# Two token groups side by side in the gate and value products of the last FFN chunks, with a new order

## The chip, the cores and the metric

The kernel runs on one NeuronCore of a Trainium2 chip. The metric is the device time of one execution in microseconds (us); the number that is compared is the median over runs. The engines are TensorE (PE, matrix products; PEld is its weight load), VectorE (DVE), ScalarE (ACT), GpSimd (POOL) and SyncE (SP), whose queue issues the DMAs here. Each runs its own list of instructions in order.

## What is computed

The reference is a linear attention with a complex decay, followed by a gated feed-forward network (FFN), all in fp32:

```python
def _attn_ref(q, k, v, a_re, a_im):          # (4, 8, 768, 48) each
    mag = np.sqrt(a_re * a_re + a_im * a_im)
    scale = np.minimum(mag, 0.999) / (mag + 1e-06)
    ...
    for t in range(S):
        new_re = ar * S_re - ai * S_im
        new_im = ar * S_im + ai * S_re
        kv = np.einsum('bhd,bhe->bhde', k[:, :, t], v[:, :, t])
        S_re, S_im = (new_re + kv, new_im)
        y[:, :, t] = np.einsum('bhd,bhde->bhe', q[:, :, t], S_re)

def _moe_ref(x, w_gate, w_val, w_out):       # x (3072, 384), d_ff 1536
    g = x @ w_gate
    silu = g * (1.0 / (1.0 + np.exp(-g)))
    val = x @ w_val
    return (silu * val @ w_out).astype(np.float32)
```

## The kernel before

**Tiling.** The 3072 tokens are 24 slabs of 128 (four batches, six pieces of the sequence). Two slabs make a group, so there are 12 groups of 256 tokens. `stage_ops(g)` prepares a group's decays, keys and queries, mostly on DVE and ACT. `slab_ops(n)` does the attention of slab n. From slab 6 on, DVE transposes its keys and queries (L650) into a spare weight tile, twelve DMAs carry that into a T tile (L659, steps sh0 to sh3; the T tag has two buffers), and PE makes the scores (`sc`, L692 into p_ps), the product with the state (`st`) and the product with the values (`V`, L692 into p_py). Between scores and values DVE multiplies with the mask (`mk`, L720). ACT copies the result, rounded, to xh (`evh`, L781); DVE makes the rest, xl (`evl`, L788). Two groups' xh and xl fit at a time.

**FFN.** `ffn_ops(g)` runs the FFN of a group in 12 chunks f of 128 hidden units. f1 (L943) makes gate and value of 256 tokens in one PSUM bank, p_gv (two of these): 18 products of 256 columns. Each fp32 operand stands as a high and a low part of the type fp32r, so a product is three: high x high, high x low, low x high, over three k-tiles. Group 0 uses plain fp32 and has 6 products instead of 18. Then follow silu on ACT (`th`, L949), the product with the value on DVE (`h2`, L954), the split of the result into `hh` (DVE or ACT) and `hl` (DVE), and f2 (L977), six products of 384 columns that add to the group's two PSUM banks p_po. After chunk 11 the two halves are copied to ost (two buffers) and stored (L991). A chunk or slab is named by group and number: f1_10.1 is chunk 1 of group 10, sc0_23 the first half of slab 23's scores.

**Weights.** At the start the weight words are converted on DVE and split into high and low parts (casts `c4` on DVE or ACT, rests `c5` on DVE). In the rest of the program the weights are read again and their range is looked at (`kl`, `k1`, `k2`, L891 to L900).

**What sets the order.** All steps are added to a `Planner`. It gives each engine, step by step, the ready step with the earliest due time (`key`, plus an entry in the table `NUDGE`), with its own prices for the steps, and then the program is written out in that order. Where a step may run on more than one engine, the planner also picks that. So constants at the head of the file move instructions anywhere in the program.

```python
pl.add("f1_" + I, {"PE": 2.16 if g else 2.6}, f1, ...)
pl.add("f2_" + I, {"PE": 1.06 if g else 1.31}, f2, ...)
slots = dict(qs=1, ks=1, T=2, dec=3, sc=2, sg=2, hh=2, hl=2, ost=2, xh=2, xl=2, vt=2, vr=2,
             gv=2, po=1, ps=2, py=1, pm=1)
```

Of the kernel before, what the change touches and what calls it, by code (L numbers as in the profile page):

```python
# [33 lines left out]
SWITCH_KEY = 6.4577  # L34
RUSH, WARY = 100.0, 8.0
CALM_S, CALM_C, CALM_T, CALM_A, CALM_D = 3.5883, 1.0641, 0.128, 0.29, 0.2775
LATE, WARY2, WARY3, WARY4 = 2.1401, 2.0386, 1.7902, 0.0841
STRETCH = 1.757
AHEAD, YIELD, QUEUED = -15.9216, 13.0268, 5.6794
T0, PER, FT, FT0 = 49.2709, 22.663, 4.032, 4.936  # L40
LEAD0, LEAD2 = 8.1674, 2.0456
CONV0, CONVP = 32.3335, 40.5772
T1 = T0 + 12 * FT0
CK0, CKP = 169.077, 13.465
RCP, SQR = 1, 2
NUDGE = {
# [13 lines left out]
SHY = -5.6765  # L60
POOL_FROM = 9.8274
# [169 lines left out]
def quick(ctx, tc, q, k, v, a_re, a_im, w_gate, w_val, w_out, out, count):  # L231
# [89 lines left out]
    def new(tag, inst):  # L321
# [6 lines left out]
        else:  # L328
# [7 lines left out]
            if tag in ("xh", "xl", "hh", "hl"):  # L336
# [591 lines left out]
    def ffn_ops(g):  # L928
        t0, step = (T1 + (g - 1) * NF * FT, FT) if g else (T0, FT0)
        for f in range(NF):  # L930
            I = f"{g}.{f}"
            key = t0 + f * step

            def f1(e, f=f, I=I):
                xh, xl = at_["xh", g], at_.get(("xl", g))
                gv = new("gv", I).rearrange("p (i t) -> p i t", i=2)
                for i, nm in enumerate(("g", "v")):
                    wh, wl = (weight(nm, f, x) for x in ((HIGH, LOW) if g else (WHOLE, WHOLE)))
                    mm = []
                    for kt in range(KT):  # L940
                        mm += [(wh[:, kt, :], xh[:, kt, :])] if g == 0 else [(wh[:, kt, :], xh[:, kt, :]), (wh[:, kt, :], xl[:, kt, :]), (wl[:, kt, :], xh[:, kt, :])]
                    for m, (l, r) in enumerate(mm):
                        nc.tensor.matmul(out=gv[:, i, :], lhsT=l, rhs=r, start=(m == 0), stop=(m == len(mm) - 1))  # L943
            pl.add("f1_" + I, {"PE": 2.16 if g else 2.6}, f1,
                   deps=[f"ev{'l' if g else 'h'}{2 * g + i}" for i in range(2)] + [f"c{5 if g else 3}{f}w", f"f1_{g}.{f - 1}", f"f1_{g - 1}.{NF - 1}"],
                   alloc=[("gv", I)], use=[("xh", g), ("xl", g)] if g else [("xh", g)], key=key)

            def silu(e, I=I):
                nc.scalar.activation(out=new("sg", I), in_=at_["gv", I][:, 0:2 * P], func=AF.Silu)  # L949
            pl.add("th_" + I, {"ACT": 0.28}, silu, deps=["f1_" + I], alloc=[("sg", I)], use=[("gv", I)], table="silu")  # L950

            def h2(e, I=I):
                sg = at_["sg", I]
                nc.vector.tensor_tensor(out=sg, in0=sg, in1=at_["gv", I][:, 2 * P:4 * P], op=ALU.mult)  # L954
            pl.add("h2_" + I, {"DVE": 0.34}, h2, deps=["th_" + I], use=[("sg", I), ("gv", I)])

            def hh(e, I=I):
                cast(e, new("hh", I), at_["sg", I])
            if g > 0:
                pl.add("hh_" + I, {"DVE": 0.2, "ACT": 0.28}, hh, deps=["h2_" + I], alloc=[("hh", I)], use=[("sg", I)], port=True)  # L960

            def hl(e, I=I):
                tt(e, new("hl", I), at_["sg", I], at_["hh", I].bitcast(F32), ALU.subtract)
            if g > 0:
                pl.add("hl_" + I, cost(("DVE", "POOL"), 2 * P), hl, deps=["hh_" + I], alloc=[("hl", I)], use=[("sg", I), ("hh", I)])

            def f2(e, f=f, I=I):
                hh, hl, h = (at_.get((x, I)) for x in ("hh", "hl", "sg"))
                products = ((hh, HIGH), (hh, LOW), (hl, HIGH)) if g else ((h, WHOLE),)
                if f == 0:  # L970
                    new("po", f"{g}.0")
                    new("po", f"{g}.1")
                for i in range(2):
                    cs = slice(i * P, (i + 1) * P)
                    po = at_["po", f"{g}.{i}"][:, :DM]
                    for j, (l, part) in enumerate(products):
                        nc.tensor.matmul(out=po, lhsT=l[:, cs], rhs=weight("o", f, part),  # L977
                                         start=f == 0 and j == 0, stop=f == NF - 1 and j == len(products) - 1)
# [259 lines left out]
```

## Time and profile before

| | |
|---|---|
| median of 3 runs | 627.1 us (626.94 to 627.57) |
| span of the profiled execution | 625.2 us |
| PE busy | 599.1 us, 96% |
| PE weight loads busy | 565.9 us, 91% |
| DVE busy | 501.6 us, 80% |
| ACT busy | 405.2 us, 65% |

The profile shows one execution. The weight load overlaps the products, so the two rows of PE are not added. Matmul records follow each other pipelined: a record of 280 ns may start 114 ns after the one ahead of it, so what a product costs is read from the distance of starts, or from a block's time in the chain of waits divided by its products. The median stands 1.9 us above the profiled span.

### The profile page before, as it was taken

Reading aid. Unit: us, or ns where it says so; the run is one execution under the profiler, and the core shown is the slowest. Engines: PE = TensorE matmul, PEld = TensorE weight load, DVE = VectorE, ACT = ScalarE, POOL = GpSimd, SP = SyncE. Lnnn points to the kernel's source line nnn. Section 1 sums busy time; section 2 is a strip of 40 time slices with the busy share of each in tenths; the row PEclk is TensorE's granted clock in tenths of the full one; section 3 lists DMA queues with packets and bytes.
Section 4 is the critical chain, followed back from the end, with each engine's and each line's share of the span. In section 5 each row is a group of like instructions: output and inputs, shape, how many; then the busy total and the mean of one; then the engine's idle time right before and its main releaser. Section 6 shows DMA issues by size and latency. Waiting matters only on the chain.

```text
span 625.2 us, 16113 instructions
## 1 busy us (share of the span) xinstructions
PE 599.1 (96%) x6562; PEld 565.9 (91%) x6562; DVE 501.6 (80%) x931; ACT 405.2 (65%) x653; POOL 4.2 (1%) x15
## 2 busy tenths in 40 slices
PE   2699999999999999999999999999999999999996
PEld 1488788989999999999999999999999999999995
DVE  8999999999978788977979869769869768544432
ACT  7953548887895885957876966966966874212210
POOL 2000000000000000000000000000000000000000
PEclk9899999999999999999999999999999999999998
DMA  7899701334544564455356354554463542331100
GB/s 257 230 280 296 246 27 33 65 123 123 142 118 124 141 153 119 129 141 127 101 144 161 114 140 108 143 142 107 132 170 103 155 109 70 102 104 51 52 1 30
DMA packets 155574, 79.89 MB, mean 128 GB/s; under 512 B 116187, under 2 KB 151261, under 8 KB 155494
## 3 DMA queue, kind: packets, MB, share of 16 engines
q1 hardware_dynamic: 155494, 78.80, 46.0%
q8 instruction: 53, 0.87, 0.6%
q14 instruction: 27, 0.22, 0.1%
HBM read 59.83 MB, written 4.78 MB: 103 GB/s over the span
## 4 chain that ended last, share of the span: by engine, by line
PE 79%; DVE 12%; DMA 3%; SPq 3%; issue 1%; ACT 1%; DVEq 0%
PE p_gv L943 41%; PE p_po L977 21%; PE p_py L692 6%; PE p_ps L692 5%; DVE ww L350 2%; PE p_pm L503 2%; PE p_pm L761 2%; DVE sg L954 1%; PE p_pm L758 1%; DMA wo<-in_q_dram 1%; SPq L681 1%; DVE s L350 1%; DVE ks L350 1%; DVE wo L350 1%; PE p_gv L630 1%
## 5 line engine op out<-in xcount | busy, mean ns | idle before, releaser
L943 PE MATMUL p_gv<-xh,ww 128*128 128x256 f32 x1596 | 303.3, 288 | 2.0 <-DVE sg L954 1.4
L943 PEld LDWEIGHTS p_gv<-xh,ww 128*128 128x128 f32 x1596 | 256.0, 189 | 9.2 <-DVE sg L954 2.9
L943 PE MATMUL p_gv<-xl,ww 128*128 128x256 f32 x726 | 201.3, 277 | 0.0
L1069 ACT ACT_TABLE_LOAD x118 | 151.4, 1283 | 2.1
L943 PEld LDWEIGHTS p_gv<-xl,ww 128*128 128x128 f32 x726 | 136.3, 188 | 0.2 <-issue 0.2
L949 ACT ACTIVATE sg<-p_gv 128x256 f32<-128x256 f32 x144 | 55.1, 385 | 122.1 <-PE p_gv L943 120.8
L977 PE MATMUL p_po<-wo,hh 128*128 128x384 f32 x484 | 125.1, 339 | 0.0
L954 DVE TENSOR_TENSOR sg<-sg,p_gv 128x256 f32<-128x256 f32 x144 | 59.0, 412 | 56.0 <-ACT sg L949 55.7
L977 PEld LDWEIGHTS p_po<-wo,hh 128*128 128x128 f32 x484 | 81.2, 188 | 1.6 <-issue 1.6
L977 PE MATMUL p_po<-wo,hl 128*128 128x384 f32 x242 | 80.8, 334 | 0.6 <-DVE hl L350 0.6
L350 DVE TENSOR_TENSOR hl<-sg,hh 128x256 fp32r<-128x256 f32 x132 | 54.8, 416 | 7.0 <-ACT hh L354 1.8
L977 PEld LDWEIGHTS p_po<-wo,hl 128*128 128x128 f32 x242 | 45.4, 188 | 0.9 <-DVE hl L350 0.9
L407 ACT ACTIVATE s<-s 128x768 f32<-128x768 f32 x44 | 36.7, 843 | 9.7 <-DVE s L350 6.7
L692 PEld LDWEIGHTS p_ps<-T 96*64 96x64 f32 x768 | 35.9, 138 | 5.0 <-issue 2.2
L692 PE MATMUL p_ps<-T 96*64 96x128 f32 (+1 forms) x768 | 39.4, 254 | 0.0
L720 DVE TENSOR_TENSOR sc<-p_ps,turn 128x512 f32<-128x512 f32 x48 | 31.8, 684 | 3.7 <-PE p_ps L692 3.5
L781 ACT CAST xh<-p_py 128x384 fp32r<-128x384 f32 x22 | 10.6, 480 | 33.9 <-PE p_py L692 33.8
L354 ACT CAST hh<-sg 128x256 fp32r<-128x256 f32 x45 | 18.1, 405 | 18.5 <-DVE sg L954 14.7
L356 DVE CAST hh<-sg 128x256 fp32r<-128x256 f32 x87 | 25.1, 290 | 6.1 <-PE p_po L977 2.5
L692 PE MATMUL p_py<-sc,vr 128*32 128x128 f32 x384 | 26.1, 273 | 0.0
L692 PE MATMUL p_py<-sc,vt 128*32 128x128 f32 x384 | 25.0, 273 | 0.0
L943 PE MATMUL p_gv<-xh,ww-1_292 128*128 128x256 f32 x132 | 24.9, 280 | 0.0
(146 smaller groups left out, 852.3 us busy)
## 6 DMA issues: line engine op xcount, KB each, us to landing
T<-ww SPq DMA_DIRECT2D x216, 64.0 KB, 2.1
wo<-in_moe_w_out_dram SPq DMA_DIRECT2D x24, 384.0 KB, 4.7
ww<-in_moe_w_gate_dram SPq DMA_DIRECT2D x12, 384.0 KB, 5.9
ww<-in_moe_w_val_dram SPq DMA_DIRECT2D x12, 384.0 KB, 6.9
vt<-in_v_dram SPq DMA_DIRECT2D x24, 192.0 KB, 4.0
out_dram<-ost SPq DMA_DIRECT2D x24, 192.0 KB, 2.2
wo<-in_moe_w_gate_dram SPq DMA_DIRECT2D x12, 384.0 KB, 5.4
wo<-in_moe_w_val_dram SPq DMA_DIRECT2D x12, 384.0 KB, 3.5
```

Of the source, the lines that this page charges most:

```text
L350: V[e].tensor_tensor(out=out, in0=a, in1=b, op=op)
L354: nc.scalar.copy(out=out, in_=in_)
L356: nc.vector.tensor_copy(out=out, in_=in_)
L407: nc.scalar.activation(out=of(to or dst), in_=of(source), func=func, scale=scale, **kw)
L503: nc.tensor.matmul(out=ps, lhsT=tri, rhs=flat(half(x, i)), start=j == 0, stop=j == 1)
L692: nc.tensor.matmul(out=o, lhsT=l, rhs=r, start=opens, stop=closes, tile_position=(0, width * slot), skip_group_check=True)
L720: nc.vector.tensor_tensor(out=s.rearrange("p (r m) t -> p r m t", m=2), in0=scores[qd].rearrange("p (r m) t -> p r m t", m=2), in1=m, op=A ...
L943: nc.tensor.matmul(out=gv[:, i, :], lhsT=l, rhs=r, start=(m == 0), stop=(m == len(mm) - 1))
L949: nc.scalar.activation(out=new("sg", I), in_=at_["gv", I][:, 0:2 * P], func=AF.Silu)
L954: nc.vector.tensor_tensor(out=sg, in0=sg, in1=at_["gv", I][:, 2 * P:4 * P], op=ALU.mult)
L977: nc.tensor.matmul(out=po, lhsT=l[:, cs], rhs=weight("o", f, part), start=f == 0 and j == 0, stop=f == NF - 1 and j == len(products) - 1)
L1069: nc.scalar.preload_act_table_set(op.load)
```

## The change

Chunks 0, 1 and 11 of groups 10 and 11 stay as they are. For chunks 2 to 10 (`PAIRED`) both groups are taken together. The xh of both groups are copied side by side into a T tile that attention no longer needs, and the same for xl (`both`, two copies each). The gate of a chunk (f1g) is nine products of 512 columns into one p_gv bank, the value (f1v) nine into the other. silu, h2, hh and hl then work on 512 columns and use the tiles of the staged attention (re, im, s1, s2, s3, qt) in place of sg, hh and hl. f2 stays at 384 columns, one step for each group. Group 10 adds up in p_po, group 11 in the two banks that held the scores. The table of due times and nudges is another one throughout.

```diff
+PAIRED = (2, 11)
...
 NUDGE = {
-    "sadd0.1": -5.6, "cumF1.1": 3.8, "mk1_3": 15.5, "c32w": 4.0, "c110w": 3.4, "f1_0.2": -12.1, "h2_0.5": 9.1,
...
+    "cumF1.1": 6.6, "c32w": 4.9, "r05": 61.6, "qs1_5": -10.4, "ld_im6": -43.0, "kz1s0": -46.3, "f2_9.0": 28.7,
...
+            if tag == "T" and isinstance(inst, str):
+                t = work.tile([P, math.prod(shape[1:])], F32R, name=inst, tag=tag, bufs=slots[tag])
+                t = t[:, INPUT:INPUT + KT * 4 * P].rearrange("p (k n) -> p k n", k=KT)
...
+    last = NGRP - 2, NGRP - 1
+    tail = [((g,), f) for g in last for f in range(PAIRED[0])] + [(last, f) for f in range(*PAIRED)]
+    tail += [((g,), f) for g in last for f in range(PAIRED[1], NF)]
...
+    def sums(g, i):
+        return scores[i].rearrange("p h t -> p (h t)")[:, :DM] if g == last[1] else at_["po", f"{g}.{i}"][:, :DM]
...
+        def gated(x, parity):
+            if many == 1:
+                return new(x, I)
+            tag, inst = {"sg": (("re", "im"), "sg"), "hh": (("s1", "s2"), "him"), "hl": (("s3", "qt"), "lim")}[x]
+            t = new(tag[parity], (inst, I))
+            at_[x, I] = flat(t)[:, GATED:GATED + wide]
+            return at_[x, I]
...
+        def product(nm, o):
+            xh, xl = (at_["xh", g], at_.get(("xl", g))) if many == 1 else (at_["T", x] for x in ("both xh", "both xl"))
+            wh, wl = (weight(nm, f, x) for x in ((HIGH, LOW) if g else (WHOLE, WHOLE)))
+            mm = []
+            for kt in range(KT):
+                mm += [(wh[:, kt], xh[:, kt])] if g == 0 else [(wh[:, kt], xh[:, kt]), (wh[:, kt], xl[:, kt]), (wl[:, kt], xh[:, kt])]
+            for m, (l, r) in enumerate(mm):
+                nc.tensor.matmul(out=o, lhsT=l, rhs=r, start=(m == 0), stop=(m == len(mm) - 1))
...
+            gate, value = ("gv", I + "gate"), ("gv", I + "value")
+            made = []
+            for i, x in enumerate(("gate", "value")):
+                made.append(pl.add(f"f1{x[0]}_" + I, {"PE": 2.05}, lambda e, i=i, x=x: f1_wide(e, i, x), deps=ready + made,
+                                   alloc=[(gate, value)[i]], use=inputs_, key=key + 2 * i))
...
+    def both(x):
+        for n, g in enumerate(last):
+            def copy(e, n=n, g=g):
+                if n == 0:
+                    new("T", "both " + x)
+                cast(e, at_["T", "both " + x][:, :, 2 * P * n:2 * P * (n + 1)], at_[x, g])
...
+    def ffn_tail(before):
+        for x in ("xh", "xl"):
+            both(x)
+        t = T1 + (NGRP - 3) * NF * FT
+        for gs, f in tail:
+            ffn_ops(gs, f, t, before)
+            t += FT * len(gs)
+            if f == NF - 1:
+                rows_out(gs[0], t + 4, before)
```

**PE, the chunks of the last groups.** Before, one chunk (f1, then f2 of the chunk ahead; L943 is f1, L977 f2):

```order
L943 MATMUL p_gv<-xh,ww_1140 128x256
L943 MATMUL p_gv<-xl,ww_1140 128x256
L943 MATMUL p_gv<-xh,ww_1140 128x256 x2
...
L977 MATMUL p_po<-wo_1127,hh 128x384 x2
L977 MATMUL p_po<-wo_1127,hl 128x384
```

Now, chunk 3's gate (L977 is f1 here, L1037 f2; p_ps are the score banks, in which group 11 adds up), behind group 11's f2 of chunk 1 and chunk 2's value:

```order
L1037 MATMUL p_ps_98<-wo_900,hh 128x384 x2
L1037 MATMUL p_ps_98<-wo_900,hl 128x384
...
L977 MATMUL p_gv<-both xh,ww_855 128x512
...
L977 MATMUL p_gv<-both xh,ww_879 128x512
L977 MATMUL p_gv<-both xl,ww_879 128x512
L977 MATMUL p_gv<-both xh,ww_879 128x512 x2
```

A gate or a value is nine instructions of 512 columns, 162 in all, where 324 of 256 stood; behind f1g of a chunk comes f2 of the chunk ahead for group 10, behind f1v the same for group 11. The whole tail of PE now reads, by the steps' names: sc and V of slab 22, f2_10.0, f1_10.1, sc and V of slab 23, f2_10.1, f1_11.0, f1_11.1, f2_11.0, f1g of chunk 2, f2_11.1, f1v, f1g of chunk 3, f2 of chunk 2 for group 10, f1v, and so on to f1v of chunk 10; then f1_10.11, f1_11.11 and the f2 that are left. Before, slab 22 stood behind f1_10.3 and slab 23 behind f1_10.7. The transposes of slab 22 stood behind f1_9.9 on DVE's side of the plan, now they stand ahead of f1_9.7.

**DVE, around slab 23's masks** (L720, now L726, into sc). Before:

```order
L954 TENSOR_TENSOR sg<-sg,p_gv 128x256
L720 TENSOR_TENSOR sc<-p_ps_98,turn 128x512
L720 TENSOR_TENSOR sc<-p_ps_99,turn 128x512
L895 TENSOR_REDUCE flags<-wo_1384 128x1
L788 TENSOR_TENSOR xl<-p_py,xh 128x3x128
```

Now:

```order
L1011 TENSOR_TENSOR sg<-sg,p_gv 128x256
L362 CAST hh<-sg 128x256
L356 TENSOR_TENSOR hl<-sg,hh 128x256
L726 TENSOR_TENSOR sc<-p_ps_98,turn 128x512
L726 TENSOR_TENSOR sc<-p_ps_99,turn 128x512
L901 TENSOR_REDUCE flags<-wo_1384 128x1
L794 TENSOR_TENSOR xl<-p_py,xh 128x3x128
L362 COPY both xl<-xl 128x3x256
```

The chunk whose f1 stands ahead of the scores has its hh and hl ahead of the masks now, and behind them before.

**DVE, the end.** Before (p_po_7857 is the second half of group 11's sums):

```order
L954 TENSOR_TENSOR sg_8160<-sg_8160,p_gv_8131 128x256
L356 CAST hh_8171<-sg_8160 128x256
L1014 CAST count_58<-p_pm_8163 1x1
L350 TENSOR_TENSOR hl_8174<-sg_8160,hh_8171 128x256
L356 COPY ost_8184<-p_po_7857 128x384
```

Now (p_po_7338 is the second half of group 10's sums, p_ps1 of group 11's):

```order
L1011 TENSOR_TENSOR sg_7924<-sg_7924,p_gv_7895 128x256
L362 CAST hh_7933<-sg_7924 128x256
L362 COPY ost_7937<-p_po_7338 128x384
L356 TENSOR_TENSOR hl_7940<-sg_7924,hh_7933 128x256
L1102 CAST count_58<-p_pm_7942 1x1
L362 COPY ost_7952<-p_ps1_99 128x384
```

Group 10's last copy came into the last chunk's steps; before, group 10 was stored nine chunks earlier. On SP the last two stores are that of ost_7952 (second half, copied by DVE) and then that of ost_7954 (first half, copied by ACT); before, the first half's went first. The two ost buffers are taken in turn: ost_7952 follows group 10's first half, ost_7954 its second.

**The start.** Up to the FFN of group 2 the order of PE is nearly the same. In what the planner gave to DVE or ACT, the casts of five 384-column and two 768-column weights, three hh and one T copy went from DVE to ACT, and two, three, one and one went from ACT to DVE.

## Rows read from the trace of the kernel before

**Rows 1.** The page's first section: busy us (share of the span) xinstructions.

```profile
PE 599.1 (96%) x6562; PEld 565.9 (91%) x6562; DVE 501.6 (80%) x931; ACT 405.2 (65%) x653; POOL 4.2 (1%) x15
```

**Rows 2.** Busy time by stretch: length, each engine's (instructions), granted clock, DMA share, GB/s.

```profile
30.00:170.00 140.00, 137.40 (x1278) 120.51 (x1274) 138.16 (x241) 94.81 (x147) 0.00 (x0) 1.00 0.52 150
225.00:450.00 225.00, 225.00 (x2828) 220.26 (x2828) 187.45 (x350) 168.76 (x256) 0.00 (x0) 1.00 0.50 130
450.00:550.00 100.00, 99.94 (x1190) 97.52 (x1189) 74.03 (x135) 59.96 (x109) 0.00 (x0) 1.00 0.44 118
550.00:600.00 50.00, 50.00 (x457) 49.60 (x456) 22.00 (x58) 10.07 (x29) 0.00 (x0) 1.00 0.19 59
```

**Rows 3.** PE's waits from 150 to 620 us: total us, times, longest.

```profile
PE p_gv L943 <- DVE sg L954: 1.4, 2, 0.9
```

**Rows 4.** Chain that ended last: start us, us, what (group 0's f1; slab 23; a chunk).

```profile
65.67 2.59 PE p_gv L943 x12
...
562.31 1.55 PE p_ps L692 x24
563.86 1.93 PE p_py L692 x64
...
567.04 2.06 PE p_gv L943 x18
569.10 1.04 PE p_po L977 x6
```

**Rows 5.** DVE by form, 30 to 170 us: xcount | busy us, mean ns | idle before.

```profile
L356 DVE CAST wo<-wo 128x384 fp32r<-128x384 f32 x7 | 2.4, 350 | 0.0
L356 DVE CAST ww<-ww 128x768 fp32r<-128x768 f32 x4 | 2.2, 544 | 0.0
L356 DVE CAST hh<-sg 128x256 fp32r<-128x256 f32 x7 | 2.0, 280 | 0.0
L650 DVE STREAM_TRANSPOSE ww<-ks 128x768 f32<-128x768 f32 x1 | 1.0, 965 | 0.0
```

**Rows 6.** Timeline around slab 23: start us, us, engine, line, what [idle before, releaser].

```profile
562.77 0.42 DVE L954 TENSOR_TENSOR sg<-sg,p_gv 128x256 f32<-128x256 f32 x1 [1.40 <-ACT sg L949]
563.22 1.39 DVE L720 TENSOR_TENSOR sc<-p_ps,turn 128x512 f32<-128x512 f32 x2
...
565.73 0.61 PE L977 MATMUL p_po<-wo,hh 128*128 128x384 f32 x2
565.86 0.48 ACT L781 CAST xh<-p_py 128x384 fp32r<-128x384 f32 x1 [2.59 <-PE p_py L692]
...
566.37 0.56 DVE L788 TENSOR_TENSOR xl<-p_py,xh 128x384 fp32r<-128x384 f32 x1 [1.30 <-ACT xh L781]
...
566.90 0.29 DVE L356 CAST hh<-sg 128x256 fp32r<-128x256 f32 x1
...
567.29 0.43 DVE L350 TENSOR_TENSOR hl<-sg,hh 128x256 fp32r<-128x256 f32 x1
```

**Rows 7.** Timeline of SP's queue: slab 22's twelve copies, the last nine of slab 23's.

```profile
530.92 8.63 SPq L659 DMA_DIRECT2D T<-ww  x12
...
549.04 6.45 SPq L659 DMA_DIRECT2D T<-ww  x9
```

**Rows 8.** The page's DMA issues: KB each, median us from issue to landing.

```profile
T<-ww SPq DMA_DIRECT2D x216, 64.0 KB, 2.1
```

**Rows 9.** Timeline of the end (columns as in rows 6).

```profile
615.32 0.28 PE L943 MATMUL p_gv<-xh,ww 128*128 128x256 f32 x1
...
616.58 0.29 DVE L356 CAST hh<-sg 128x256 fp32r<-128x256 f32 x1
...
619.06 1.34 SPq L991 DMA_DIRECT2D out_dram<-ost  x2
619.07 0.56 DVE L356 COPY ost<-p_po 128x384 f32<-128x384 f32 x1 [1.75 <-PE p_po L977]
```

**Rows 10.** The 24 stores of L991, from issue to landing.

```profile
DMA to landing us min/median/max: 1.9/2.2/6.5
```

More of the change, by code (lines that the diff above doesn't have):

```diff
@@ L59 @@
 HIGH, LOW, WHOLE = 0, 1, 2
-SHY = -5.6765
-POOL_FROM = 9.8274
+SHY = -83.4065
+POOL_FROM = -45.6425
 TABLES = {"exp": ("exp_and_others", "natural_log_exp_and_others"), "ln": ("natural_log_exp_and_others",),
@@ L925, in sector_ops @@
             pl.add(f"km{i}{N}", STT2, least, deps=[f"kz{i}{N}"], use=parts, key=key)
[L928 to L967, printed above, removed]
@@ new lines, in banks, with ffn_ops, home, f1 @@
+    def banks(g):
+        return [("ps", f"sums{i}") for i in range(2)] if g == last[1] else [("po", g)]
+    def ffn_ops(gs, f, key, before):
+        g, many = gs[0], len(gs)
+        I = name(gs, f)
+        wide = 2 * P * many
+        def gated(x, parity):
[5 more added lines that the diff above has]
+            return at_[x, I]
+        def home(x):
+            if many == 1:
+                return x, I
+            tag, inst = {"sg": (("re", "im"), "sg"), "hh": (("s1", "s2"), "him"), "hl": (("s3", "qt"), "lim")}[x]
+            return tag[f % 2], (inst, I)
+        def product(nm, o):
[6 more added lines that the diff above has]
+                nc.tensor.matmul(out=o, lhsT=l, rhs=r, start=(m == 0), stop=(m == len(mm) - 1))
+        def f1(e):
+            gv = new("gv", I).rearrange("p (i t) -> p i t", i=2)
+            for i, nm in enumerate("gv"):
+                product(nm, gv[:, i, :])
+            at_["gate", I], at_["value", I] = gv[:, 0], gv[:, 1]
+        def f1_wide(e, i, x):
+            at_[x, I] = new("gv", I + x)
+            product("gv"[i], at_[x, I])
+        ready = [f"ev{'l' if g else 'h'}{2 * g_ + i}" for g_ in gs for i in range(2)] + [f"c{5 if g else 3}{f}w"] + before["f1"]
+        inputs_ = [(x, g) for x in ("xh", "xl")[:2 if g else 1]]
+        if many > 1:
+            inputs_ = [("T", "both " + x) for x in ("xh", "xl")]
+            ready += [f"both {x}{g_}" for x in ("xh", "xl") for g_ in gs]
+        if many == 1:
+            gate = value = ("gv", I)
+            product_ = pl.add("f1_" + I, {"PE": 2.16 if g else 2.6}, f1, deps=ready, alloc=[gate], use=inputs_, key=key)
+            made = [product_] * 2
+        else:
+            gate, value = ("gv", I + "gate"), ("gv", I + "value")
[3 more added lines that the diff above has]
+                                   alloc=[(gate, value)[i]], use=inputs_, key=key + 2 * i))
+        def silu(e):
+            nc.scalar.activation(out=gated("sg", f % 2), in_=at_["gate", I], func=AF.Silu)
+        pl.add("th_" + I, {"ACT": 0.28 if many == 1 else 0.5}, silu, deps=[made[0]], alloc=[home("sg")], use=[gate], table="silu")
+        def h2(e):
+            sg = at_["sg", I]
+            nc.vector.tensor_tensor(out=sg, in0=sg, in1=at_["value", I], op=ALU.mult)
+        pl.add("h2_" + I, {"DVE": 0.34 if many == 1 else 0.61}, h2, deps=["th_" + I, made[1]], use=[home("sg"), value])
+        def hh(e):
+            cast(e, gated("hh", f % 2), at_["sg", I])
+        def hl(e):
+            tt(e, gated("hl", f % 2), at_["sg", I], at_["hh", I].bitcast(F32), ALU.subtract)
+        if g > 0:
+            pl.add("hh_" + I, {"DVE": 0.2, "ACT": 0.28} if many == 1 else {"DVE": 0.34, "ACT": 0.51}, hh,
+                   deps=["h2_" + I], alloc=[home("hh")], use=[home("sg")], port=True)
+            pl.add("hl_" + I, cost(("DVE", "POOL"), wide), hl, deps=["hh_" + I], alloc=[home("hl")], use=[home("sg"), home("hh")])
+        made_ = []
+        for n, g_ in enumerate(gs):
+            opens, closes = (steps(g_)[x] == (gs, f) for x in (0, -1))
+            def f2(e, n=n, g_=g_, opens=opens, closes=closes):
@@ L976, in f2 @@
                     for j, (l, part) in enumerate(products):
-                        nc.tensor.matmul(out=po, lhsT=l[:, cs], rhs=weight("o", f, part),
-                                         start=f == 0 and j == 0, stop=f == NF - 1 and j == len(products) - 1)
-            PO = [("po", g)]
-            pl.add("f2_" + I, {"PE": 1.06 if g else 1.31}, f2,
-                   deps=([f"hl_{I}", f"c5{f}o"] if g else [f"h2_{I}", f"c3{f}o"]) + ([f"f2_{g}.{f - 1}"] if f else []),
-                   alloc=PO if f == 0 else [], use=([("hh", I), ("hl", I)] if g else [("sg", I)]) + (PO if f else []), key=key + 3)
+                        nc.tensor.matmul(out=sums(g_, i), lhsT=l[:, cs], rhs=weight("o", f, part),
+                                         start=opens and j == 0, stop=closes and j == len(products) - 1)
@@ L1049, in quick @@
         weight_ops(f)
-    ffn_ops(0)
+    before = {"f1": []}
+    ffn_group(0, before)
     for f in range(NF):
@@ L1060, in quick @@
         range_ops(f)
-    for g in range(1, NGRP):
-        ffn_ops(g)
+    for g in range(1, last[0]):
+        ffn_group(g, before)
+    ffn_tail(before)
     verdict_ops()
```

56 lines of the change are left out of this document (36 added, 20 removed), and 12 rows, old and new, of the table NUDGE.

## The prediction

> **What bounds the kernel now.** I read the page's busy shares first: TensorE (PE) is busy 96% of the span, VectorE (DVE) 80% [rows 1]. A share is a mean over stages, so the next view is the busy time by stretch [rows 2]. It shows two regimes. From 30 to 170 us DVE is busy 138.16 of 140 us: that stretch lasts as long as DVE's list of work. From 225 us on PE is busy all the time (225.00 of 225, and 50.00 of 50 near the end), the granted clock is 1.00 there (the 2.4 GHz level), and DVE has 17 to 56% to spare. The view of waits agrees: after 150 us PE waits 1.4 us in all, twice [rows 3]. So after 170 us time changes by what PE has to execute and by new waits of PE. The chain of waits gives PE's prices [rows 4]: a chunk's 18 gate and value products of 256 columns (f1) take 2.06 us, its 6 output products of 384 columns (f2) 1.04, a slab's scores 1.55 and its states and values 1.93. The profiled execution spans 625.2 us; the median of the three timed runs is 627.1, 1.9 above it. I add each change to 627.1.
>
> **The 512 columns.** Chunks 2 to 10 of groups 10 and 11 were 18 f1 blocks of 18 products, 324 products of 256 columns in 18 x 2.06 = 37.1 us, or 114 ns each. They become 162 products of 512. No 512-column product is in the trace. Lower bound: in group 0 the operands are plain fp32, and each f1 product leaves two records (12 records for 6 instructions). They follow each other in 2.59 / 12 = 216 ns [rows 4], which is about what 512 columns take at one column a cycle of 2.4 GHz (213 ns). Upper bound: the 384-column products take 1.04 / 6 = 174 ns, in proportion 232 ns for 512. I take 217, the fp32 row's price, for this reason: where PE never waits, its weight loads are busy 49.60 of 50 us [rows 2], so a product of 256 columns seems to wait for its weights, and a longer one would not. Gain: 37.1 - 162 x 0.217 = 1.9 us. At 216 it is 2.1, at 232 it is a loss of 0.5.
>
> The rows give 114 ns for 256 columns, 228 for two of them. The Trainium skill (TensorE: Matmul & The Clock Gate, Back-to-back issue gap) gives an isolated product N / 2.4 + 2.5 ns: 109 for 256 and 216 for 512. By that rule alone two short products cost 218 and the gain would be 162 x 2.7 ns = 0.4 us, an estimate from that page. The trace's 114 contradicts its first half; whether the second holds for these operands no run here shows yet.
>
> **What comes with them.** The silu, product and splits of a wide chunk work on 512 columns. Their lengths can at most double: on DVE h2 0.42, hh 0.29, hl 0.43 [rows 6], so 2.3 us, 2.7 with the gaps between. The order puts one f2 and the next chunk's gate product (1.04 + 1.95) between a value product and the f2 that needs its hl, so this is hidden. Only for chunk 2 there is the gate product alone, 1.95 us, and of its f2 the first two products need hh only: 0 to 0.4, taken as 0.1. The four copies that lay both groups' xh and xl side by side ("both") are ACT and DVE work of under 1 us each (a cast of 768 columns is 0.54 on DVE [rows 5]). Two f1 and one f2 of group 11 (5.2 us) stand between them and the first wide product. If that cover were gone, they would cost some 2 us.
>
> **What moves: slabs 22 and 23.** The wide chunks need both groups' tokens, so 22 f1 and 23 f2 now follow slab 23's value product, where 16 and 19 did: 6 x 2.06 + 4 x 1.04 = 16.5 us of PE work. Slab 23's scores come that much earlier. Before, its twelve copies into T were issued by 555.5 and landed 2.1 us later, at 557.6 [rows 7, 8], 4.6 us before its scores at 562.2 [rows 4]. In the new order slab 22's transposes stand at f1 of chunk 9.7, and 7 f1, 8 f2 and two slabs (29.7 us) separate that from slab 23's scores. In these must go, by my placing from the rows: transposes done at 1.5, twelve copies 8.6, landing 2.1; slab 23's transposes behind hl of chunk 9.9, at 14.8 to 16.8 (0.97 each [rows 5]); copies and landing until 27.5. Some 2 us remain. On DVE about 9 us of group 11's stage moves ahead of slab 21. Between 450 and 550 DVE idles 26 us of 100 [rows 2], so there is room, but its load before slab 21 rises from 83% to some 95%. I add 0.2 us for short waits, with 0 to 2.5 as bounds.
>
> **Slab 23's mask.** DVE's order now has hh and hl of chunk 10.1 ahead of the masks; before, only h2 stood there. Before, h2 ended at 563.19 and the masks 563.22 to 564.61, and the values ran to 565.73 [rows 6]. With 0.29 + 0.43 and their gaps of 0.1 the masks end 0.7 to 0.95 later, and the second half of the values (from about 565.25) waits 0.1 to 0.35. Taken: 0.3. Then group 11's f1 wants xh and xl: they were ready at 566.93, 1.2 us after the values [rows 6], and f2 of chunk 10.1 covers 1.04 of that and f1's first product the rest: 0.
>
> **The last stores.** Group 10's outputs now close two f2 before group 11's. There are two ost buffers, so each last copy waits until a store of group 10 has landed, and the order of the last two stores is turned round. Count from the start of the last f1 product (615.32 before [rows 9]). DVE's hh ended at 1.55; the copy of group 10's second half now stands behind it (0.56), so its store goes out at 2.14 and lands after 2.2 (least 1.9 [rows 10]), at 4.34. Then ACT's last copy, 0.48 as the 384-column cast [rows 6], and the last store is issued at 4.85. Before, it was issued when DVE's copy was done, 619.63, at 4.31. Cost 0.5 us; 0.2 with the shortest landing, 1.2 if the two stores delay each other by 0.6.
>
> **The ramp.** Between 30 and 170 us, where DVE sets the time, the new plan gives five 384-column and two 768-column weight casts, three hh and one T copy to ACT, and takes two, three, one and one back: net 3 x 0.35 + 2 x 0.28 - 0.54 = 1.1 us less on DVE [rows 5]. PE's order up to there is nearly the same. The recorded lengths overlap a little, so I take 0.8 us. Bounds: 1.7 gained, 0.5 lost, since the places of many steps shift too.
>
> **Sum.** -1.9 + 0.1 + 0.2 + 0.3 + 0.5 - 0.8 = -1.6 us, so 627.1 becomes 625.5.
>
> **Rivals.** (1) *Eaten up.* The 1.9 us are there, but the ramp gives nothing and the new waits come at their upper bounds: -1.9 + 0.4 + 0.35 + 1.2 + 0.2 = +0.2, so 627.3. For it: three of the waits are new in the order and need no bad luck. Against it: all at once. (2) *A 512-column product costs as the 384-column one does*, 232 ns: +0.5 in place of -1.9, so 628.0. For it: all 384-column products here, whatever they read, take 174 ns and not 163. Against it: the fp32 row. (3) *Slower: slab 23 comes late.* Its scores wait for T, because DVE's transposes for slabs 22 and 23 slip. My account leaves 2 us, so each microsecond of slip beyond 2 is one lost; with the other terms at -1.6, a slip of 5 us gives 628.5 and of 6 us 629.5. For it: 83% to 95% load on DVE and one queue (SP) for the 24 copies, the check loads and the stores. Against it: from 225 to 450 us DVE ran at 83% with PE never idle. (4) That the products stay 256 wide is out: the built order shows 162 of 512.
>
> **How the numbers follow.** A measurement here can tell about 0.2%, 1.25 us, from no change: 625.85 and 628.35. The forecast (624 to 626.5) has 0.50; it straddles the lower mark, and I put 0.43 below it. Rival 1 has 0.26, rival 2 0.08, both within the marks; rival 3 has 0.16, of which 0.13 beyond the upper one. So faster has 0.43, same 0.07 + 0.26 + 0.08 + 0.03 = 0.44, slower 0.13; the forecast itself is the likeliest case. Range: from 623.8 (512 columns at 216 ns, ramp 1.7, the waits 0.5 together) to 628.4, which takes in rivals 1 and 2 and part of 3.
>
> **What would show it.** In the new profile: wide f1 products 215 to 220 ns apart and 1.95 us a block (232 ns would be rival 2). PE idle at slab 23's scores with T or the transposes as the releaser (rival 3), or only at its values, for 0.3 us, with the mask as the releaser (forecast). The last store issued 4.5 to 5.5 us after the last f1 product. The chain leaving DVE near 169 us in place of 170. I am wrong if PE is idle more than 2 us in all after 230 us, or if the stretch up to 170 us got longer.

## The result and the profile after

The changed kernel takes 630.6 us (630.45 to 631.2, four runs) against 627.2 for the kernel before on the same chip: a ratio of 1.0059, 95% interval 1.0047 to 1.0072, so 3.5 us slower by the medians where 1.6 us faster was forecast, and above the upper end of the stated range, 628.4. The profiled execution spans 628.8 us, 3.6 more than before. The page's first section and the busy time by stretch, in the columns of [rows 1, 2]:

```profile
PE 600.3 (95%) x6400; PEld 560.4 (89%) x6400; DVE 499.6 (79%) x909; ACT 391.8 (62%) x634; POOL 4.2 (1%) x15
```

```profile
30.00:170.00 140.00, 137.17 (x1277) 121.03 (x1274) 137.63 (x238) 91.92 (x147) 0.00 (x0) 1.00 0.53 151
225.00:450.00 225.00, 224.71 (x2818) 219.54 (x2817) 188.18 (x350) 162.62 (x252) 0.00 (x0) 1.00 0.50 127
...
550.00:600.00 50.00, 50.00 (x278) 43.89 (x272) 18.05 (x39) 10.20 (x23) 0.00 (x0) 1.00 0.13 40
```

The picture of the two regimes is the same. The last row holds the first surprise: between 550 and 600 us the weight loads (PEld) fell from 49.60 busy microseconds to 43.89, as was meant, and PE is as busy as ever. The chain of waits around slab 23 and the first wide blocks says what that bought (to be read beside [rows 4]):

```profile
547.19 1.55 PE p_ps L698 x24
548.74 2.21 PE p_py L698 x64
550.96 1.24 PE p_po L1037 x6
552.20 4.19 PE p_gv L977 x36
556.39 1.04 PE p_ps L1037 x6
557.43 2.10 PE p_gv L977 x9
559.53 1.05 PE p_ps L1037 x6
560.58 4.20 PE p_gv L977 x18
```

Nine products of 512 columns take 2.10 us, 233 ns each, and not 1.95. A gate and a value block, 18 products, take 4.20 us. 36 products of 256 columns, as many as such a pair replaces, take 2 x 2.06 = 4.12 by [rows 4]; the fourth line, 4.19, is group 11's f1 of chunks 0 and 1, still 256 columns wide, which lose 0.08 us at the first product with xl (xl was just ready then).

To place the rest I compare ends of steps before which TensorE has the same work in both kernels, or correct for f1 and f2 that have changed sides at 2.06 and 1.04 us. Up to slab 6's values the changed kernel is 0.2 us ahead (191.9 against 192.1). The 1532nd step of both plans is f1 of chunk 7.5, and the 1532 steps up to there are the same set; it starts at 414.92 us in the changed kernel and 413.48 in the one before: 1.4 behind. At slab 22's values it is still 1.4, at slab 23's 1.7. From there to the last product of the output the changed kernel loses 0.9 more (2.6), and from that product to the end of the span 1.1 (7.5 against 6.5 us). So: **order 1.4, slab 23 0.3, wide chunks 0.9, end 1.1**, 3.6 in all.

### The profile page after: what moved, and what is told of

Same layout as the page of the kernel before. It is cut to its first block, busy times and chain, and to the rows that moved or that the text cites. A ratio compares the mean times of both kernels' runs of the same rounds, so it can differ in the third digit from the quotient of the medians.

```text
span 628.8 us, 15712 instructions
## 1 busy us (share of the span) xinstructions
PE 600.3 (95%) x6400; PEld 560.4 (89%) x6400; DVE 499.6 (79%) x909; ACT 391.8 (62%) x634; POOL 4.2 (1%) x15
## 4 chain that ended last, share of the span: by engine, by line
PE 83%; DVE 9%; ACT 3%; DMA 2%; issue 2%; SPq 1%; DVEq 0%; ACTq 0%
PE p_gv L977 43%; PE p_po L1037 20%; PE p_py L698 6%; PE p_ps L698 6%; PE p_pm L767 2%; PE p_pm L509 2%; PE p_ps L1037 2%; PE p_gv L636 2%; DVE ww L356 1%; DVE sg L1011 1%; ACT L1159 1%; PE p_pm L764 1%; DVE s L356 1%; DMA dr<-qs 1%; DVE ks L356 1%
## 5 line engine op out<-in xcount | busy, mean ns | idle before, releaser
L977 PE MATMUL p_gv<-xh,ww 128*128 128x256 f32 x1380 | 263.8, 289 | 3.1 <-DVE sg L1011 2.5
L977 PEld LDWEIGHTS p_gv<-xh,ww 128*128 128x128 f32 x1380 | 222.5, 189 | 10.4 <-DVE sg L1011 4.0
L977 PE MATMUL p_gv<-xl,ww 128*128 128x256 f32 x618 | 171.6, 278 | 0.0
L977 PEld LDWEIGHTS p_gv<-xl,ww 128*128 128x128 f32 x618 | 116.1, 188 | 0.0
L1037 PE MATMUL p_po<-wo,hh 128*128 128x384 f32 x404 | 104.6, 340 | 0.0
L1011 DVE TENSOR_TENSOR sg<-sg,p_gv 128x256 f32<-128x256 f32 x126 | 51.3, 411 | 30.8 <-ACT sg L1006 30.0
L1037 PEld LDWEIGHTS p_po<-wo,hh 128*128 128x128 f32 x404 | 68.3, 188 | 1.4 <-issue 1.2
L1037 PE MATMUL p_po<-wo,hl 128*128 128x384 f32 x202 | 67.6, 335 | 0.0
L1037 PEld LDWEIGHTS p_po<-wo,hl 128*128 128x128 f32 x202 | 37.9, 188 | 0.1
L977 PE MATMUL p_gv<-both xh,ww 128*128 128x512 f32 x108 | 36.7, 395 | 0.0
L726 DVE TENSOR_TENSOR sc<-p_ps,turn 128x512 f32<-128x512 f32 x48 | 31.8, 686 | 3.5 <-PE p_ps L698 3.3
L906 ACT ACTIVATE wo<-wo 128x384 f32<-128x384 f32 x36 | 20.0, 556 | 9.2 <-DMA wo<-in_moe_w_gate_dram 5.7
```

Of the source, the lines that this page charges most:

```text
L726: nc.vector.tensor_tensor(out=s.rearrange("p (r m) t -> p r m t", m=2), in0=scores[qd].rearrange("p (r m) t -> p r m t", m=2), in1=m, op=A ...
L906: nc.scalar.activation(out=high(0), in_=high(1), func=AF.Square, accum_out=flags[:, fl_hi + j:fl_hi + j + 1])
L977: nc.tensor.matmul(out=o, lhsT=l, rhs=r, start=(m == 0), stop=(m == len(mm) - 1))
L1011: nc.vector.tensor_tensor(out=sg, in0=sg, in1=at_["value", I], op=ALU.mult)
L1037: nc.tensor.matmul(out=sums(g_, i), lhsT=l[:, cs], rhs=weight("o", f, part), start=opens and j == 0, stop=closes and j == len(products) - 1)
```

## Experiments

All times are against the kernel before, run on the same chip between the runs of the experiment. Differences in us are the ratio's distance from 1 times 627; where the medians say something else, both stand. Offsets in a single trace are good to about half a microsecond at best: of kernels with the same order some are 0.9 us later than others already when slab 0 ends (34 us), before any step of the change. That end goes with TensorE's granted clock, which rises while the first groups' products run: it stays at 1.00 (the 2.4 GHz level) from 26.8 to 28.4 us on in the traces whose slab 0 ends at 33.8 to 34.2 us, and from 28.5 to 29.3 us on in those where it ends at 34.4 to 34.9.

### The same weights, two halves

```diff
-                nc.tensor.matmul(out=o, lhsT=l, rhs=r, start=(m == 0), stop=(m == len(mm) - 1))
+                for c in range(0, wide, 2 * P):
+                    nc.tensor.matmul(out=o[:, c:c + 2 * P], lhsT=l, rhs=r[:, c:c + 2 * P],
+                                     start=(m == 0 and c == 0), stop=(m == len(mm) - 1 and c + 2 * P >= wide))
```

> The changed kernel, but each product of 512 columns is issued as two of 256 with the same weights, one behind the other; order, tiles and all other work as in the changed kernel. Theory C (a product of this type costs by its columns, 0.46 ns each, whatever its weights do): the halves follow each other in 114 ns, a pair of blocks takes 4.10 us in place of 4.20, 162 x 5 ns = 0.8 us come back, 629.8 us. Rival W (the 233 ns are the wide operand's own price: it lies in a longer tile and is written by other casts): the halves read the same tile and take 116 to 117 ns each, 630.6 us. Rival L (a short product waits for its weight load, as the prediction took it): the halves take 114 ns, but a second half whose weights are there already is shorter, and the time falls by more than 0.8 us.

Ratio 1.0035 (1.0022 to 1.0047), 2.2 us above before, where the changed kernel was 3.7 above by its ratio; by the medians it is 2.7 and 3.5. So 0.8 to 1.5 us came back, and the time alone does not tell theory C from rival L. The chain of this run, and two rows of its timeline inside a block:

```profile
558.24 2.06 PE p_gv L978 x18
560.30 1.04 PE p_ps L1038 x6
561.34 4.10 PE p_gv L978 x36
```

```profile
561.01 0.36 PEld L978 LDWEIGHTS p_gv<-both xh,ww 128*128 128x128 f32 x2
561.18 0.40 PE L978 MATMUL p_gv<-both xh,ww 128*128 128x256 f32 x2
```

36 short products take 4.10 us where 18 long ones took 4.20, and from slab 23's values to the last product the trace is 0.8 us shorter. That is theory C's price: one wide product costs 5 ns more than two narrow ones. The second pair of rows shows what the edit does not do: each half loads its weights again (324 loads for 324 products here, 162 for 162 in the changed kernel). So half as many loads save nothing, which is shown; what two products would gain from one load that they share is not tested by this run or by any later one.

### What a product costs

> The changed kernel, with the gate and value products of chunks 3 to 8 of the last two groups issued in other cuts, all with the same order of work: chunk 3 as 2 x 256 columns, 4 as 384 + 128, 5 as 4 x 128; chunks 6, 7 and 8 on bf16 views of the same data (the upper halves of the words, so these three chunks' gates and values are computed from coarser numbers) as 512, 2 x 256 and 4 x 128. It is a measure of prices, its time is no result. Theory C (a fp32r product costs 0.455 to 0.467 ns a column at any width): 512 columns 233 ns, 256 114, 384 + 128 174 + 58, 128 columns 58. Rival L (a product takes at least the 110 ns that a weight load takes): 128 columns about 110 ns each. On bf16: if the price belongs to the type, 512 columns take 213 to 216 ns, 256 107 to 109; if it belongs to the place or to the weight loads, 233 and 114 as before.

The chain again; the blocks are chunk 2's gate (nine of 512), chunk 3's value (2 x 256), chunk 4's gate (384 + 128), chunk 5's gate (4 x 128), and the bf16 blocks of chunks 6, 7 and 8 (512, 2 x 256, 4 x 128):

```profile
558.20 2.11 PE p_gv L982 x9
...
566.65 2.05 PE p_gv L982 x18
...
569.75 2.54 PE p_gv L982 x18
...
577.00 3.97 PE p_gv L982 x36
...
590.24 2.06 PE p_gv L982 x9
...
593.34 2.06 PE p_gv L982 x18
...
599.55 2.12 PE p_gv L982 x36
```

Two things are seen. In bf16 the weight loads of 128 x 128 follow each other every 59 ns (2.12 / 36), and yet a bf16 product of 256 columns takes 114 ns, as the fp32r product does. So in bf16 it is not the weights that set 114, and the same price in fp32r speaks against them there too. And the fp32r product of 128 columns takes 110 ns and not 58: below 256 columns something else sets it, and theory C alone is too simple. The next run tells what.

> The changed kernel with nine products more ahead of each wide gate and value block of chunks 3 to 9, whose sums are overwritten by the block. They tell width of the weights from width of the columns (weights x columns): chunk 3 128 x 128, chunk 4 64 x 128, chunk 5 32 x 128, chunk 6 32 x 256, chunk 7 128 x 192, chunk 8 32 x 512, chunk 9 128 x 320. Its time is no result. Theory L' (a fp32r product takes the longer of its columns, 0.45 ns each, and its weight load, 110 ns for 128 weight columns): 128 x 128 110 ns, 64 x 128 and 32 x 128 58 ns, 32 x 256 114, 128 x 192 110, 32 x 512 233, 128 x 320 146. Theory N (fp32r products under 256 columns run at a lower rate whatever the weights): 128 columns 110 ns with 32 weight columns too, 192 columns 165 or 110.

The added products have a line of their own, L980, nine to a block; in order 128 x 128, 64 x 128, 32 x 128, 32 x 256, 128 x 192, 32 x 512, 128 x 320:

```profile
563.40 0.95 PE p_gv L980 x9
...
571.70 0.54 PE p_gv L980 x9
...
579.16 0.53 PE p_gv L980 x9
...
586.63 1.05 PE p_gv L980 x9
...
595.00 0.98 PE p_gv L980 x9
...
603.27 2.08 PE p_gv L980 x9
...
613.74 1.32 PE p_gv L980 x9
```

That is 106, 60, 59, 117, 109, 231 and 147 ns. With 64 or 32 weight columns, 128 columns cost 60; with 128 weight columns, 128 and 192 columns both cost 106 to 109; at 256 and 512 columns 32 weight columns are no cheaper (117 and 231) than 128 (114 and 233). Theory L' holds in all seven: **a fp32r product takes the longer of its columns at about 0.455 ns and its weight load of about 108 ns**. The two meet at some 240 columns (an estimate, 108 / 0.455), so the 256 columns of the kernel before were already past the point from which a weight load is hidden.

The Trainium skill has this number (TensorE: Matmul & The Clock Gate, LDWEIGHTS): a load takes its weight columns divided by 1.2 ns, 107 for 128. The 106 measured here agrees. Set beside the 114 of [rows 4], it would have taken away my reason to expect a gain.

### The order and the pairing, one at a time

The constants and the table of nudges are exchanged between the two kernels, nothing else.

> The kernel before with the constants and the table of nudges of the changed kernel, and no wide products. Its planned order is that of the changed kernel on TensorE up to f1 of chunk 7.5 (about 390 us), and the end has before's form. Theory O (the order that came with the change loses 1.2 to 1.5 us before 390 us by itself, and the wide products and the end the rest): 628.3 to 628.8 us. Rival (the order costs nothing, the whole loss is made where the wide products are): 627.2 us. What the prediction took: the ramp gains 0.8, 626.4 us.

> The changed kernel with the constants and the table of nudges of the kernel before. Its planned order is that of the kernel before on TensorE up to f2 of chunk 8.2 (about 430 us); the pairing stands behind it. Theory C and O: the stretch up to 430 us is as before, the wide products cost 0.75 us, the stores at the end 0.5 to 1.1, slab 23's masks 0 to 0.3: 628.4 to 629.4 us. Rival (the wide products gain 1.9 and only the order lost): 625.5 to 626.5 us. If the order of the changed kernel was needed for the pairing, slab 23 comes late and the time is over 630.

The new table alone: 1.0076 (1.0059 to 1.0094), 4.8 us lost, more than any theory had. Up to f1 of chunk 7.5 it is as expected (414.79 us without the sum that stands ahead of it here, 1.3 behind). Then comes a wait of 2.8 us for a h2 up to 502 us, in a stretch where this kernel's order is that of neither kernel, and it costs more than its length. During the wait TensorE's granted clock falls from 1.00 to 0.50 (the 1.2 GHz level), and the f1 behind it takes 4.21 us in place of 2.06; with the scores (2.40 for 1.55) that is 3.0 us more. The clock is the last number but two of the first row:

```profile
501.30:508.10 6.80, 6.03 (x42) 5.81 (x44) 4.62 (x10) 1.84 (x5) 0.00 (x0) 0.50 0.86 194
```

```profile
502.07 4.21 PE p_gv L945 x18
```

So the total says nothing of the changed kernel. The pairing alone: 1.025 (1.023 to 1.027), 16 us. Its longest wait of TensorE from 530 to 600 us, SP's queue before it, and the chain behind it (slab 23):

```profile
PE p_ps L696 <- DMA T<-ww: 5.7, 1, 5.7
```

```profile
547.45 6.67 SPq L663 DMA_DIRECT2D T<-ww  x9
```

```profile
555.91 2.79 PE p_ps L696 x24
558.70 3.29 PE p_py L696 x64
```

The last nine copies of slab 23's T are issued until 554.1 and slab 23's scores wait 5.7 us for them. Here too the granted clock falls during the wait (0.50 from 554.6 to 561.4 us, the 1.2 GHz level), and slab 23 takes 6.1 us in place of 3.5. Four waits for h2 after 150 us make 3.8 us, where the kernel before has 1.4 in two. Together that is 10.7 us of the 16 lost; the wide products and a later end bring some 3 more, and the rest is not placed. The wait for T is rival 3 of the prediction, in this order and not in that of the changed kernel: the pairing needs slab 23 some 15 us earlier, and of the orders tried here only the new table's gets it there in time. What that costs elsewhere is the next question.

### The end and the masks

```diff
+    for what, ahead_of in (("hh_10.1", "V23"), ("hl_10.1", "V23"), ("oe11.0", "oe11.1"), ("os11.0", "os11.1")):
+        op = pl.by[what]
+        order.remove(op)
+        order.insert(order.index(pl.by[ahead_of]), op)
...
-                t = work.tile(shape, dt, name=tag, tag=tag, bufs=slots[tag])
+                t = work.tile(shape, dt, name=tag, tag=tag, bufs=3 if tag == "ost" else slots[tag])
```

> The changed kernel with two places of its order mended: hh and hl of chunk 10.1 stand behind slab 23's masks on VectorE; and there are three ost buffers in place of two, with the last two copies and stores in the old order (ScalarE's first). Theory E (both places cost what the trace shows: 0.28 us of TensorE idle at slab 23's values, and 1.06 us longer from the last product to the end): the values take 1.93 us again, the end takes 6.5 us from the last product, together 1.3 us back, 629.3 us. Rival (the end is long because four stores lie close together, not because of the buffer): 0.3 us back, 630.3 us.

Ratio 1.0037 (1.0023 to 1.0051): 1.4 us better than the changed kernel, where theory E has 1.3. First the masks. The timeline of the changed kernel at slab 23, then the chain of this run:

```profile
548.10 0.29 DVE L362 CAST hh<-sg 128x256 fp32r<-128x256 f32 x1
...
548.43 0.42 DVE L356 TENSOR_TENSOR hl<-sg,hh 128x256 fp32r<-128x256 f32 x1
...
548.77 1.28 DVE L726 TENSOR_TENSOR sc<-p_ps,turn 128x512 f32<-128x512 f32 x2
...
550.10 0.11 PEld L698 LDWEIGHTS p_py<-sc,vt 128*32 128x32 f32 x2 [0.15 <-DVE sc L726]
```

```profile
548.88 1.93 PE p_py L698 x64
```

hh and hl ahead of the masks, the second half of the values behind them: 2.21 us; without them 1.93 as before. Then the end, of the changed kernel (first) and of this run:

```profile
621.78 0.48 ACT L360 COPY ost<-p_ps 128x384 f32<-128x384 f32 x1 [2.62 <-DMA out_dram<-ost]
622.27 1.98 SPq L1055 DMA_DIRECT2D out_dram<-ost  x2
```

```profile
621.14 0.48 ACT L360 COPY ost<-p_ps 128x384 f32<-128x384 f32 x1 [1.94 <-PE p_ps L1037]
621.66 0.98 SPq L1055 DMA_DIRECT2D out_dram<-ost  x2
```

ScalarE's copy waited for a store of group 10 to land; with a third buffer it waits for TensorE alone, and the last two stores go out at 621.66 to 622.64 and not 622.27 to 624.25. From the last product to the end it is 6.15 us, in the changed kernel 7.54. The run changes the buffers and the order of the last two stores together, so how the gain at the end divides between the two is not shown.

### The old order up to 415 us

The first 1532 steps are put in the order of the kernel before, with its engines; the rest stays.

> The changed kernel, but the first 1532 of its steps (up to f1 of chunk 7.5, about 415 us) stand in the order and on the engines of the kernel before; from there on its own order, pairing and end. At that point both orders have done the same set of steps. Theory O (the order before the pairing loses 1.2 to 1.5 us): 629.2 us, values of slab 16 at the time of the kernel before, wide products, masks and end as in the changed kernel. Rival (the order up to there costs nothing that lasts, the loss is made later): 630.6 us.

Ratio 1.0027 (1.0013 to 1.0041): 2.0 us better than the changed kernel by the ratios, 1.1 by the medians, where theory O had 1.4. The time of one step in the trace would not show it: this execution was 0.8 us late when slab 0 ended, and f1 of chunk 7.5 starts at 415.15. So I read stretches. From slab 6's values to f1 of chunk 7.5 the changed kernel and the runs of the halves, of the new table and of the mended end take 1.5 to 1.7 us longer than the kernel before (the two runs on prices 1.2 and 1.4), those with the old order 0.1 to 0.5. Part of the spread comes from waits for h2 near 208 us, which differ from run to run. From the last product of slab 8's values on, where the kernel before has no wait, the same products up to that f1 take 176.9 to 177.1 us in all eight traces with the old order there and 178.0 to 178.6 in all six with the new one (in the new table's run without the sum that stands early there): 1.4 us in the mean. From slab 0's values to slab 6's, the ramp, the two orders don't differ: against the kernel before, -0.2 to +0.1 us with the new one, -0.5 to +0.3 with the old one in other runs. The run that settles it cuts at slab 6:

> As the kernel with all four causes taken back, but its first 717 steps (up to the values of slab 6, 192 us) stand in the new order and only steps 718 to 1532 (192 to 415 us) in the old one. In the traces so far the new order takes 1.5 to 1.7 us longer from slab 6's values to f1 of chunk 7.5 than the kernel before, 0.7 of it in a stop inside slab 14's values, and the old one 0.1 to 0.5. Theory M (the order's loss lies in the steps between 192 and 415 us): that stretch takes at most 0.5 us longer than in the kernel before, slab 14's values have no stop, and the time is that of the kernel before or up to 0.5 us less, 626.5 to 627.5. Rival (the loss follows from the new ramp, as buffers and transfers stand otherwise when it ends): the stretch is 1.5 us longer again, 628.5 us.

Ratio 1.0005 (0.9996 to 1.0014), the time of the kernel before. The chain of this run, of the kernel before and of the changed kernel at f1 of chunk 7.5:

```profile
413.55 2.06 PE p_gv L1083 x18
```

```profile
413.48 2.06 PE p_gv L943 x18
```

```profile
414.92 2.06 PE p_gv L977 x18
```

The loss lies in the order of the steps between 192 and 415 us, as theory M says. About half of it has one place, the values of slab 14, in five of the six traces with the new order (here the changed kernel and the one with the end mended):

```profile
362.81 0.39 PE L698 MATMUL p_py<-sc,vr 128*32 128x128 f32 x4
363.49 0.30 PE L698 MATMUL p_py<-sc,vr 128*32 128x128 f32 x1 [0.29 <-issue]
```

```profile
363.18 0.30 PE L698 MATMUL p_py<-sc,vr 128*32 128x128 f32 x1 [0.43 <-issue]
```

TensorE stops between two products, 0.55 to 0.71 us from one to the next, after both masks are done (361.9) and with no wait that the trace knows ("issue"). No kernel with the old order has it. The sixth trace with the new order, of the run on prices in other cuts, does not have it either (0.13 us at that place), so the order alone does not bring it; that trace is still 1.1 us longer in the stretch. What stops TensorE stays open. One thing stands beside it in the traces: a fetch of instructions (queue q8, 16 KB, one for about 250 records of TensorE and its weight loads) lands at 361.8 to 362.4 us in all six, 1.2 to 1.5 us ahead of the product behind the stop; with the old order the last such landing lies 2.4 us or more ahead of the same product. An engine that runs short of instructions would look like this; no run tests it. Of the changed kernel's 1.4 us the slabs' values hold 0.7, nearly all of it in slab 14; the rest is spread thinly over many f1 blocks (0.5) and f2 blocks (0.2).

### Everything taken back but the pairing

> All four causes taken back while the pairing stays: the old order up to 415 us, products of 2 x 256 columns with the same weights, hh and hl of chunk 10.1 behind slab 23's masks, three ost buffers with the last stores in the old order. Theory (the loss is the sum of order 1.2 to 1.5, width 0.8, masks 0.3, end 1.0 to 1.4, and nothing else): 626.7 to 627.5 us, the time of the kernel before. Rival (something else in the pairing costs, such as the copies or 512-column work on VectorE and ScalarE): 628 us or more. Rival L (the shared weights gain something): below 626.5.

Ratio 0.9987 (0.9971 to 1.0002). The medians are equal (627.6). With the old order up to 415 us, halves, masks and end mended, the pairing has no cost or gain clear of the noise: from 1.8 us gained to 0.1 lost by the interval. The four causes together account for the loss; the four "both" copies and the work on 512 columns of VectorE and ScalarE are hidden. For rival L there is no sign: the interval's middle is 0.8 us, but the trace's blocks are 2.06 us as ever. As in the first run each half loads its own weights, so a load that is really shared is not tested here either.

### A side track: waits of the kernel before

> The kernel before with two steps moved: the silu of chunk 3.0 ahead of the sine of stage 4 on ScalarE and its product h2 ahead of ks1 of stage 4 on VectorE. In the trace of before TensorE waits 1.1 us at 208.5 us for that h2; the sine waits 2 us for a transfer, with the silu behind it. Theory (after 170 us each microsecond of TensorE idle is one of time): 1.0 us less, 626.1 us. Rival (the wait turns up again at the next chunk, as VectorE has the sine's users late anyway): 627.2 us.

> The kernel before with the two moves of the silu and h2 of chunk 3.0, and h2 of chunk 3.1 ahead of qs1 of stage 4, h2 of chunk 2.3 ahead of the flag reduction k10, all on VectorE. The first two moves alone gave 0.5 us in the trace at 208 us and left a wait of 0.8 us at 210.3 us. Theory: 0.5 + 0.75 + 0.47 us of TensorE's waits go, 625.5 us against 627.2. Rival (each wait is handed to the next chunk, VectorE being full up to 215 us): no more than 0.5 us.

> The pairing with its four causes taken back (old order up to 415 us, products of 2 x 256 columns, masks and end mended) and the four moves as well. Theory (the parts add): 1.7 us less than the kernel before, 625.5 us. Rival: within 0.5 us of the kernel before.

The first gave 0.9993 (0.9979 to 1.0008): not told apart from nothing; in its trace 0.8 us of the wait turned up again one block later, at 210.3, much as the rival said. With all four moves 0.9985 (0.9974 to 0.9996), 0.9 us less than before of the 1.7 expected, the one version here that is faster than both kernels, if barely. TensorE's waits between 150 and 230 us in that run, which were 1.4 us before [rows 3]:

```profile
PE p_gv L943 <- DVE sg L954: 0.5, 1, 0.5
```

The paired kernel with the same moves has a median 1.1 us below before, but one run of it was 634.8 us and its interval is 0.9973 to 1.0021: undecided. In its trace two waits of 1.7 us together remain at 210 and 214 us, so the moves did not do there what they did in the kernel before.

## Why the prediction was wrong, point by point

- **What bounds the kernel: right.** After 170 us TensorE sets the time, and each of the four losses shows at the end, in full within the noise. The marks that I set for being wrong (2 us of TensorE idle after 230 us, a longer stretch up to 170) were not reached, and the sum was wrong all the same: they watched for waits, not for the price of a product.
- **The 512 columns: wrong, and the largest miss.** The step is "I take 217, the fp32 row's price, for this reason: ... a product of 256 columns seems to wait for its weights". The price is 233, rival 2's 232, which had a chance of 0.08. In place of -1.9 the term is +0.7 (18 blocks of 2.10 us for 18 of 2.06); the first experiment gave 0.8 of it back. Two readings failed. The fp32 row is of another kind of product: a record of it takes 216 ns, a fp32r or bf16 product of 512 columns 229 to 233. And weight loads that are busy 99% of a stretch do not say that products wait for them: a load's record is 188 ns long there, while the run on the price floor had a product and a load of this size every 106. The rows of the same type had the answer: 114 for 256 columns and 174 for 384 are 0.445 and 0.453 ns a column, a line through zero, on which no weight load shows.
- **What the skill's gap gave.** The figure of the Trainium skill for an isolated product of 512 columns (TensorE: Matmul & The Clock Gate, Back-to-back issue gap), 216 ns, which no run had shown then, does not hold for the products here: 233 in fp32r, 229 in bf16. The measurement decides.
- **What comes with the wide chunks: right.** 0.1 was taken for chunk 2's f2, and the chain shows none (1.05 us for 1.04). Group 11's first two f1, taken at 0, lose a little at the first product with xl: 4.19 for 4.12.
- **Slabs 22 and 23: right that T comes in time**, with nothing lost at the scores. Slab 23's copies were issued until 542.5 us and its scores began at 547.2; with 2.1 us to the landing that leaves 2.6, where the account had some 2. Rival 3 needed another order, and there it cost 5.7 us of waiting and 2.6 of the lower clock behind it.
- **Slab 23's mask: right** in mechanism and size, 0.28 for 0.3.
- **The last stores: mechanism right, size half.** The last store was to be issued 4.85 us after the start of the last f1 product, and was, at 4.8. But the account ended with the issue; the two stores, now 0.4 us apart, took 1.98 us to issue and not 1.34 [rows 9], and the end came 1.1 later and not 0.5.
- **The ramp: wrong.** -0.8 was taken, and nothing came: from slab 0 to slab 6 the changed kernel gains 0.1 us, no more than kernels of one order differ. VectorE had 0.5 us less work up to 170 us [rows 2], where 1.1 was reckoned, but idled as much more; that it is busy 98% of a stretch does not make the stretch as long as its list. The chain leaves it at 169.8 us and not near 169; from 166.8 to 169.3 it runs through ScalarE, where it stayed on VectorE before. TensorE got a new wait there. The f1 at which the chain passes to TensorE, before and now, and that wait:

```profile
170.03 1.97 PE p_gv L943 x15
```

```profile
169.82 2.21 PE p_gv L977 x17
```

```profile
161.79 0.39 PE L977 MATMUL p_gv<-xh,ww 128*128 128x256 f32 x1 [0.76 <-DVE sg L1011]
```

- **What was not in the sum: 1.6 us between 192 and 415 us** in this trace, 1.4 in the mean of the traces of either order from slab 8 on. The prediction looked for moves where the pairing works and in the ramp, and put the steps between at nothing, with no reason given. A new table can move any step; a full engine has no slack to take that up, and any new stop is time. No rival held this cost: the prediction's own terms, with rival 2's price, no gain in the ramp and the end as measured, come to 629.3 (627.1 + 0.5 + 0.1 + 0.2 + 0.3 + 1.1).

Sum with the measured terms: +0.9 (wide chunks, all from slab 23's values to the last product) + 1.4 (order up to slab 22) + 0.3 + 1.1 = 3.7, against 3.6 in the traces and 3.5 in the medians. Two slips in the prediction change nothing: rival 2's time is 627.9 and not 628.0, and the gap rule's gain for a pair is 2.5 ns and not 2.7.

## What to carry to other kernels

Before products are made wider to save weight loads, take the price per column from two widths of the same operand type: if they lie on a line through zero, the loads are hidden already and there is nothing to save. A busy share of weight loads near 100% is no proof that they bind: a load's record (188 ns here) can be longer than what the load costs (106). And when a planner's constants change together with an idea, price the whole new order, or carry the idea into the old order first: here the idea gave no gain clear of the noise, and its new order cost 1.4 us.

## What the runs showed of the hardware that I had not expected

- A fp32r product with 128 weight columns takes 106 to 110 ns at 128 columns as at 192: four of 128 columns cost 3.97 us a block where two of 256 cost 2.06. With 64 weight columns 128 columns take 60.
- In bf16 the same products of 128 x 128 follow in 59 ns, so cutting them narrow is nearly free there (2.12 us a block for 2.06). The Trainium skill (TensorE: Matmul & The Clock Gate, Weight-path perf modes) gives non-fp32 weights a faster load; these rows agree with it, and that fp32r gets none of it.
- TensorE can stop for half a microsecond in the middle of a slab's products, at the same place in five of six traces with the same order, for no reason that the trace names; a fetch of instructions landed 1.2 to 1.5 us ahead of the product behind the stop.
- A long wait of TensorE can cost twice: after 2.8 and 5.7 us without a product its granted clock was 0.50 (the 1.2 GHz level), and the work in that time took 3.0 and 2.6 us longer.
